# Four edits to the order of small work in a fused attention and mixer kernel: the pace of the weight sums, the engine of one cast, the slots of six stores, the slot of one unit

## The chip, the core and the metric

One core of a Trainium2 chip runs the whole kernel. The metric is the time of one execution in device microseconds (us), the median of several. A core has engines that run side by side, each through its own instructions in order: TensorE (PE; its weight loads are shown as PEld), VectorE (DVE), ScalarE (ACT), GpSimd (POOL), and SyncE (SP), which here only issues DMAs. They wait for each other by semaphores. TensorE writes its results to PSUM, a small memory from which VectorE and ScalarE read; everything else lies in SBUF.

## The reference

Local attention with a few global keys, and behind it a mixer: a low-rank product over the positions, then a feed-forward layer, both with a residual.

```python
batch, n_heads, seq, head_dim = (4, 8, 768, 64); n_global, n_local = (8, 96); rank = 32
# attention, for each batch and head
scores = q @ k.T / sqrt(64) - slope[h] * dist          # dist = distance, 96 for far global keys
scores = where(is_global | is_local, scores, -1e9)
x = softmax(scores) @ v                                 # -> [batch, 768, 512]
# mixer, for each batch
u = x + ((x.T @ U) @ V).T                               # U [768, 32], V [32, 768]
out = u + maximum(u @ w_ch1, 0) @ w_ch2                 # w_ch1 [512, 2048], w_ch2 [2048, 512]
```

## The kernel before

**Pairs.** The attention is done for two heads at a time: 4 batches of 4 such pairs, so pairs 0 to 15, pair `i` of batch `i // 4`. Pairs 0 to 3 (batch 0) run in a first loop. The main loop at the end of the function runs `i` from 4 to 17; in its turn `i` it does the scores of pair `i`, the product with v of pair `i - 1`, the mixer's low-rank step of pair `i - 1`, and it spreads "units" of the feed-forward layer between these steps. The order of every engine's instructions is that in which the code issues them.

**One turn of the main loop**, in its order on TensorE: scores in three parts (`st_S`, each freed for the next by VectorE's L403, which writes `sp`); between them the two halves of the product with v (`st_V`, VectorE's L437 and L451 behind it, then GpSimd's cast L452 of the result to `x16`); then `st_M1` (six matmuls, L461, x16 against U), whose small result is cast into a tile `turn16` (in the profile: `zw`) at L465; then `st_MT` (one matmul, L478, that turns it, read out at L479 into `tmp`); then `st_M3` (L515, against V, added to x at L520, after which GpSimd's L523 casts to x16); then `st_X`, a transposition by DMA (L504) of x16 into `uT`, which the feed-forward layer reads. In turns from 7 on SyncE also transposes the next pair's k and q (L327, L330). The exp of ScalarE (L415, two in a turn) needs all three parts of `sp`; ScalarE further casts k and q two pairs ahead (L129), once their loads have landed.

**Units.** `fill(n)` issues `n` units, at nine places in a turn, with the numbers of the tuple `units`. A unit is an "up" (eight matmuls, L629, u against w_ch1 into the accumulator `hps`, and a relu on ScalarE, L634) or a "down". For batch 0 a down is four matmuls of L664, and after four of these L669 adds to x. For the other batches the second product is done with seven products of sub-blocks instead of eight (L682, added at L687), for which sums of blocks are needed: sums of the activations (`s`, `htr`) for each group of 256 rows, and sums of the weights (`t1` to `t4`) once. Three PSUM accumulators rotate for `hps` and for the transposed q and k (tag "th"); the scores and M3 share one accumulator, and the product with v, M1 and MT share another.

**The weight sums.** `queue_weight_sums` puts ten VectorE operations (L553: six of 128x1024, four of 128x512) into the queue `slow`, each with a count of units from which it is due (`wait`); `fill` counts units and takes one due entry of `jobs` or else of `slow` behind each. They are queued when batch 0's second tile of rows begins, in turn 7.

**Stores.** A finished tile of 128 rows of x is stored by SyncE (L643). Batches 1 to 3 store at once. Batch 0's six stores are kept in `kept` and issued from turn 10 on, up to three a turn, ahead of `st_MT`; on SyncE's queue that is ahead of the turn's `st_X`.

Of the kernel before, what the change touches and what calls it, by code (L numbers as in the profile page):

```python
# [16 lines left out]
ALU = mybir.AluOpType  # L17
# [3 lines left out]
def kernel(  # L21
# [13 lines left out]
    nc = tc.nc  # L35
# [9 lines left out]
    R = moe_U.shape[1]  # L45
    NP = H // 2
    NPE = 2 * NP
# [36 lines left out]
    def ps_ob():  # L84
        return psum.tile([P, 512], FP32, name="ob", tag="ob", bufs=1)
# [4 lines left out]
    def ps_th(name, dtype=FP32, cols=512):  # L90
        return psum.tile([P, cols], dtype, name=name, tag="th", bufs=3)
# [5 lines left out]
    def load_qk(i, behind=None):  # L97

        b, h0 = i // NP, 2 * (i % NP)
        got = []  # L100
        for src, nm in ((q, "qst"), (k, "kst")):
            st = stp.tile([P, 2, NSB, D], FP32, name=nm, tag=nm, bufs=2)
            if behind is not None:
                behind.memset(st[0:1, 0, 0, 0:1], 0.0)
            if i < NPE:
                nc.sync.dma_start(
                    st.rearrange("p h n d -> p h (n d)"),
                    src[b, h0:h0 + 2].rearrange("h (p n) d -> p h (n d)", n=NSB),
                )
            else:  # L110
                nc.sync.dma_start(
                    st.rearrange("p h n d -> p (h n) d"),
                    src[b, h0:h0 + 2].rearrange("h (n p) d -> p (h n) d", p=P),
                )
            got.append(st)
        staged[i] = got
# [15 lines left out]
    def load_v(i):  # L132
        b, h0 = i // NP, 2 * (i % NP)
        st = stp.tile([P, 2 * NSB, D], FP32, name="vst", tag="vst", bufs=2)
        nc.sync.dma_start(
            st, v[b, h0:h0 + 2].rearrange("h (n p) d -> p (h n) d", p=P)
        )
        vsts[i] = st
# [84 lines left out]
    turn16 = [zw[:, i * P:(i + 1) * P] for i in range(2)]  # L223
# [11 lines left out]
    def new_batch(b):  # L235
        xs[b] = xp.tile([P, NSB, DM], FP32, name="x_sb", tag="x_sb", bufs=3)
        tmps[b] = xp.tile([P, DM], FP16, name="tmp16", tag="tmp16", bufs=3)
        uTs[b] = xp.tile([P, NDC, S], FP16, name="uT", tag="uT")
# [84 lines left out]
    def turn(i):  # L323
        stq, stk = cast.pop(i)
        qT = kp.tile([P, S], FP16, name="qT", tag="qT")
        kT = kp.tile([P, S], FP16, name="kT", tag="kT")
        nc.sync.dma_start_transpose(  # L327
            kT.rearrange("d (n p) -> d n p", n=NSB), stk.rearrange("p n h d -> p (n h d)")
        )
        nc.sync.dma_start_transpose(  # L330
            qT.rearrange("d (n p) -> d n p", n=NSB), stq.rearrange("p n h d -> p (n h d)")
        )
        qts[i] = qT
        kts[i] = kT
# [74 lines left out]
    def st_S(i, c):  # L409
        s_dve(i, scores(i, c, False))  # L410
# [44 lines left out]
    def st_M1(i):  # L455
        b, dc = i // NP, i % NP
        ch = slice(dc * P, (dc + 1) * P)
        if b:
            tps = ps_ob()
            for n in range(NSB):  # L460
                nc.tensor.matmul(  # L461
                    tps[:, 0:R], x16s[i][:, n], u16[:, n, 0:R],
                    start=(n == 0), stop=(n == NSB - 1),
                )
            nc.vector.tensor_copy(turn16[i % 2][:, 0:R], tps[:, 0:R])  # L465
            return
        tps = ps_th("tmp_ps")
        for n in range(NSB):
            nc.tensor.matmul(
                tps[:, 0:P], u16[:, n], x16s[i][:, n],  # L470
                start=(n == 0), stop=(n == NSB - 1),
            )
        nc.vector.tensor_copy(tmps[b][:, ch], tps[:, 0:P])
# [72 lines left out]
    jobs, slow = deque(), deque()  # L546
# [3 lines left out]
    def queue_sum(name, part, out_, a, b_, op, wait=0):  # L550

        def go():
            nc.vector.tensor_tensor(out_, a, b_, op)  # L553
            have.add((name, part))
        (slow if name[0] == "t" else jobs).append((count[0] + wait, go))
# [7 lines left out]
    def queue_weight_sums():  # L563

        t = wbig.tile([P, 3, HJ, HD], FP16, name="t16")
        b11, b12, b21, b22 = quarters
        dead = [slI[:, 0:4], slI[:, 4:8], rel16[:, 0:2], relB.bitcast(BF16)]
        dead = [d.bitcast(FP16) for d in dead]
        dead = [d if len(d.shape) == 2 else d.rearrange("p a c -> p (a c)") for d in dead]
        t3 = [d.rearrange("p (j c) -> p j c", j=2) for d in dead]  # L570
        tw.update(t1=t[:, 0], t2=t[:, 1], t3=t3, t4=t[:, 2])
        for name, a, b_ in (
            ("t1", b12, b11), ("t2", b22, tw["t1"]), ("t3", b22, b12), ("t4", b21, tw["t2"])
        ):
            for k in range(2 if name != "t3" else len(t3)):
                n = HJ // 2 if name != "t3" else HJ // len(t3)
                js = slice(k * n, (k + 1) * n)
                to = tw[name][:, js] if name != "t3" else t3[k]
                queue_sum(name, k, to, a[:, js], b_[:, js], ALU.subtract, wait=3 * len(slow))

    def weight(w, j):
        return tw[w][:, j] if w != "t3" else tw[w][j // 2][:, j % 2]
# [129 lines left out]
    ahead, held, kept = [0], [True], deque()  # L712

    def fill(n):
        for _ in range(n):
            unit()
            count[0] += 1
            for _ in range(2 if len(jobs) > 4 else 1):
                for queue in (jobs, slow):
                    if queue and queue[0][0] < count[0]:  # L720
                        queue.popleft()[1]()
                        break
# [77 lines left out]
    for i in range(NP, NPAIR + 2):  # L800
        b, hp = divmod(i, NP)
        live = i < NPAIR
        units = iter(
            (0, 1, 1, 2, 1, 1, 1, 1, 0) if i == NP
            else (0, 1, 1, 1, 1, 1, 1, 1, 1) if i + 1 < NPE
            else (1, 1, 1, 2, 1, 1, 1, 1, 1)
        )
        held[0] = i < NP + 3
        if hp == 0 and live and b + 1 < B:
            new_batch(b + 1)  # L810
        if live and i > NP:
            st_S(i, 0)
        if NPE <= i + 1 < NPAIR:
            turn(i + 1)
        if i + 1 < NPAIR and i != NP + 2:
            load_v(i + 1)
        if i + 2 < NPE:
            load_qk(i + 2)
        fill(next(units))
        if NPE + 2 <= i + 2 < NPAIR:  # L820
            cast_one(i + 2, 1, nc.scalar)
        if NP < i <= NPAIR:
            st_V(i - 1, 0)
        if i == NP:
            load_w1(2)
        if i + 1 < NPE:
            st_T(i + 1)
        if i == NP:
            load_w1(3)
        fill(next(units))  # L830
        if live:
            st_S(i, 1)
        fill(next(units))
        if NP < i <= NPAIR:
            st_V(i - 1, 1)
        if live:
            cast_v(i)
            st_A(i)
        if NPE + 2 <= i + 2 < NPAIR:
            cast_one(i + 2, 0, nc.scalar)  # L840
        if NPE <= i + 3 < NPAIR and i != NP + 2:
            load_qk(i + 3)
        if i > NP + 1 and (i - 2) % NP == NP - 1:
            queue_ff((i - 2) // NP)
            ahead[0] = 1
        if i == NPAIR + 1:
            break
        fill(next(units))
        if live:
            st_S(i, 2)  # L850
        fill(next(units))
        if i > NP:
            st_M1(i - 1)
        else:
            for xo, o, rb in later:
                nc.vector.tensor_tensor(xo, o, rb, ALU.mult)
        if i == NP + 1:
            load_w2(0)
            load_w2(1)
        if i + 2 < NPE:  # L860
            cast_qk(i + 2, nc.gpsimd)
        if live:
            st_E(i, 0)
            if i < NPE:
                st_P(i)
        fill(next(units))
        if i >= NPE + 2:
            for _ in range(min(3, len(kept))):
                kept.popleft()()
        if i > NP:  # L870
            st_MT(i - 1)
        if NPE <= i + 1 < NPAIR:
            st_K(i + 1)
        fill(next(units))
        if i > NP:
            st_M3(i - 1)
        if live:
            st_E(i, 1)
        fill(next(units))
        if i == NP + 1:  # L880
            load_v(i + 2)
            load_qk(i + 4)
        if i > NP:
            st_X(i - 1)
        if i == NP + 1:
            load_w2(2)
            load_w2(3)
        if NPE <= i + 2 < NPE + 2:
            cast_qk(i + 2, nc.gpsimd)
        fill(next(units))  # L890
# [38 lines left out]
```

## Time and profile before

| | us |
|---|---|
| median of 3 runs | 233.63 |
| the runs | 233.42, 233.63, 235.15 |
| the profiled execution, its own time | 234.27 |
| its span (first to last instruction) | 232.5 |

A turn as the profile times it, from one pair's first scores to the next's (busy time of the engines):

| pair | stretch, us | length | TensorE | VectorE | ScalarE | GpSimd |
|---|---|---|---|---|---|---|
| 8 | 73.5 to 85.1 | 11.60 | 11.60 | 9.31 | 4.80 | 5.12 |
| 9 | 85.1 to 96.5 | 11.40 | 11.40 | 9.03 | 6.15 | 2.68 |
| 10 | 96.5 to 108.8 | 12.30 | 11.53 | 11.25 | 8.86 | 3.47 |
| 11 | 108.8 to 120.2 | 11.40 | 11.31 | 9.68 | 6.97 | 2.82 |
| 12 | 120.2 to 131.4 | 11.20 | 11.20 | 9.69 | 7.88 | 2.23 |
| 13 | 131.4 to 144.7 | 13.30 | 11.71 | 10.24 | 7.97 | 3.34 |
| 14 | 144.7 to 156.2 | 11.50 | 11.37 | 10.08 | 6.16 | 2.82 |

The granted clock of TensorE is 1.0 throughout. The profile's rows give the start of an instruction from the span's start, its duration, the engine ("SPq" is SyncE's queue, where the time is that of issuing a DMA and not of its transfer), the line, the operation, what it writes and reads, and in square brackets how long the engine was idle before it and whose work ended that. Matmuls are pipelined, so a TensorE row overlaps the next one, and time is best read from start to start.

### The profile page before, as it was taken

How to read it: one execution, taken by the hardware profiler on the slowest of the kernel's cores; microseconds unless marked ns; L12 is line 12 of the kernel's file. 1: busy time of each engine (PE TensorE's matmuls, PEld its weight loads, DVE VectorE, ACT ScalarE, POOL GpSimd, SP SyncE). 2: the span in 40 equal slices, each digit the busy share in tenths (PEclk: the TensorE clock that was granted, in tenths of full speed). 3: DMA queues.
4: the chain of work that ended last, by engine and by line, in shares of the span. 5: the costliest groups of instructions: out<-in, count | busy, mean ns of one | idle time of the engine just before them, and what ended most of it. 6: DMA issues, size and time to landing. Idle time of an engine off the chain costs nothing.

```text
span 232.5 us, 5864 instructions
## 1 busy us (share of the span) xinstructions
PE 220.9 (95%) x2420; PEld 170.3 (73%) x2420; DVE 161.2 (69%) x349; ACT 123.9 (53%) x181; POOL 73.8 (32%) x118
## 2 busy tenths in 40 slices
PE   6899999899999999999999979999999999999994
PEld 2455678788745456877888858888998888888883
DVE  3687776759587968797979877979755444544452
ACT  6776857685705354957485738283633334333320
POOL 7399918297543413232313131222211000000000
PEclk9999999999999999999999999999999999999999
DMA  5999998969999978765999995861251202011022
GB/s 171 304 282 270 282 291 139 320 120 176 192 175 221 208 170 178 182 154 135 272 211 272 245 226 130 94 197 37 77 82 34 93 0 92 1 45 48 0 93 90
DMA packets 86562, 36.67 MB, mean 158 GB/s; under 512 B 74152, under 2 KB 83592, under 8 KB 86536
## 3 DMA queue, kind: packets, MB, share of 16 engines
q1 hardware_dynamic: 81480, 32.01, 57.5%
q0 software_dynamic: 5056, 4.29, 12.3%
q8 instruction: 19, 0.31, 0.6%
q14 instruction: 7, 0.06, 0.1%
HBM read 27.46 MB, written 6.29 MB: 145 GB/s over the span
## 4 chain that ended last, share of the span: by engine, by line
PE 68%; DVE 12%; DMA 8%; POOL 5%; ACT 2%; issue 1%; SPq 1%; DVEq 0%; POOLq 0%
PE hps L629 28%; PE cx L682 11%; PE cps L664 9%; PE cy L682 9%; DVE sp L403 4%; DMA vst<-in_v_dram 3%; PE sc L365 2%; DVE s L553 2%; DMA uT<-x 2%; DMA kT<-k 2%; PE sc L515 2%; PE ob L432 1%; DVE x_sb L687 1%; DVE htr L553 1%; PE ob L428 1%
## 5 line engine op out<-in xcount | busy, mean ns | idle before, releaser
L629 PE MATMUL hps<-uT,w 128*128 128x256 f16 x756 | 96.0, 273 | 1.4 <-DMA uT<-x 0.7
L634 ACT ACTIVATE htr<-hps 128x512 f16<-128x512 f32 x96 | 56.3, 597 | 60.4 <-PE hps L629 60.3
L629 PEld LDWEIGHTS <-w 128*128 128x128 f16 x756 | 70.6, 98 | 11.2 <-issue 1.6
L403 DVE SCALAR_TENSOR_TENSOR sp<-sc,relcat 128x1024 f32<-128x1024 f32 (+1 forms) x36 | 40.6, 1129 | 9.8 <-ACT ep L415 3.5
L415 ACT ACTIVATE ep<-sp 128x1408 f16<-128x1408 f32 x24 | 33.0, 1376 | 12.9 <-DVE sp L403 12.3
L452 POOL CAST x<-x_sb 128x384 f16<-128x384 f32 x30 | 16.4, 547 | 48.2 <-DVE x_sb L451 45.9
L682 PEld LDWEIGHTS <-htr 128*128 128x128 f16 x288 | 27.5, 98 | 4.7 <-ACT htr L634 1.1
L687 DVE TENSOR_TENSOR x_sb<-cx,x_sb 128x256 f32<-128x256 f32 x36 | 15.2, 422 | 18.1 <-PE cx L682 17.6
L523 POOL CAST x<-x_sb 128x768 f16<-128x768 f32 x12 | 10.9, 905 | 43.9 <-DVE x_sb L520 43.9
L664 PE MATMUL cps<-w,htr 128*128 128x512 f16 x96 | 24.0, 379 | 0.0
L682 PEld LDWEIGHTS <-s 128*128 128x128 f16 x216 | 20.3, 98 | 2.4
L687 DVE TENSOR_TENSOR x_sb<-cy,x_sb 128x256 f32<-128x256 f32 x27 | 11.4, 422 | 13.0 <-PE cy L682 12.7
L365 PEld LDWEIGHTS <-kT 64*128 64x128 f16 x192 | 8.3, 93 | 13.6 <-issue 12.2
L451 DVE TENSOR_TENSOR x_sb<-ob,rcp 128x384 f32<-128x384 f32 x30 | 16.7, 557 | 1.0
L365 PE MATMUL sc<-qT,kT 64*128 64x128 f16 x192 | 16.8, 221 | 0.0
L432 PE MATMUL ob<-v,ep 128*128 128x65 f16 x192 | 16.5, 193 | 0.0
L432 PEld LDWEIGHTS <-ep 128*128 128x128 f16 x192 | 13.9, 98 | 2.3 <-issue 0.3
L142 POOL CAST v<-vst 128x768 f16<-128x768 f32 x16 | 13.8, 865 | 3.9 <-DMA vst<-in_v_dram 3.9
L428 PE MATMUL ob<-vA,ep 128*128 128x65 f16 x160 | 14.4, 194 | 0.4 <-DVE vA L316 0.2
L520 DVE TENSOR_TENSOR x_sb<-sc,x_sb 128x768 f32<-128x768 f32 x12 | 11.5, 955 | 4.4 <-PE sc L515 4.4
L372 PE MATMUL sc<-qT,kA 64*128 64x128 f16 x160 | 14.3, 217 | 0.3
L664 PEld LDWEIGHTS <-htr 128*128 128x128 f16 x96 | 8.4, 97 | 8.0
(108 smaller groups left out, 310.8 us busy)
## 6 DMA issues: line engine op xcount, KB each, us to landing
qst<-in_q_dram SPq DMA_DIRECT2D x16, 384.0 KB, 5.5
kst<-in_k_dram SPq DMA_DIRECT2D x16, 384.0 KB, 5.6
vst<-in_v_dram SPq DMA_DIRECT2D x16, 384.0 KB, 3.9
out_dram<-x_sb SPq DMA_DIRECT2D x23, 256.0 KB, 3.5
w<-in_moe_w_ch_dram POOLq DMA_DIRECT2D x8, 512.0 KB, 8.0
vA<-v SPq DMA_DIRECT2D x8, 152.3 KB, 3.2
out_dram<-x_sb SPq DMA_DIRECT2D x2, 128.0 KB
uT<-x SPq DMA_TRANSPOSE x12, 3.6
```

The costliest lines, as they stand in the source:

```text
L365: nc.tensor.matmul(scs[hi][:, o:o + P], kT[r, kb * P:(kb + 1) * P], qT[r, kb * P:(kb + 1) * P], start=(o == 0 and not on_pe), stop=(o + P ...
L403: nc.vector.scalar_tensor_tensor(out=sps[i][:, :, c0:c0 + tot], in0=both[:, :, 0:tot], scalar=qk_scale / slope[2 * (i % NP)], in1=relfs[c0 ...
L415: nc.scalar.activation(eps[i][:, hi], sps[i][:, hi], AF.Exp, scale=slope[2 * (i % NP)])
L428: nc.tensor.matmul(ob[:, qi], ep[:, OF[qi - 1]:OF[qi - 1] + P], vA[:, qi - 1, hi], start=True, stop=False,)
L432: nc.tensor.matmul(ob[:, qi], ep[:, DG[qi]:DG[qi] + P], vt[:, qi, hi], start=(qi == 0), stop=True,)
L451: nc.vector.tensor_tensor(xo, ob[:, :, 0:D], rb, ALU.mult)
L452: nc.gpsimd.tensor_copy(x16, xo)
L629: nc.tensor.matmul(hps[:, k * FT:(k + 1) * FT], w1_16[:, dc, jt * P:(jt + 1) * P], uT[:, dc, ts], start=(dc == 0 and k == 0), stop=(dc == ...
L634: nc.scalar.activation(cell["htr"][:, 2 * jp:2 * jp + 2].rearrange("p j t -> p (j t)"), hps, AF.Relu)
L664: nc.tensor.matmul(cps, htr[:, jc, t * P:(t + 1) * P], w2_16[:, jc], start=(b > 0 and jc == 0), stop=(jc == NJC - 1),)
L682: nc.tensor.matmul(ps, cell[a][:, j], weight(w, j), start=(first and j == 0), stop=(done is not None and j == HJ - 1), skip_group_check=True,)
L687: nc.vector.tensor_tensor(x_sb[:, n, cs], ps, x_sb[:, n, cs], ALU.add)
```

## The change

Four edits, of which no one adds or removes arithmetic:

- `st_M1`'s cast at L465 (128x32, 12 in all) is issued on ScalarE instead of VectorE. On ScalarE it stands behind the relu of the unit ahead of M1 and ahead of the pair's first exp;
- the ten weight sums come due two units apart instead of three. In the order of VectorE's instructions the last of them moves from pair 10 to pair 9, and the earlier ones move up through pairs 7 to 9;
- batch 0's six stores are issued in turns 8, 9 and 10, up to two a turn. On SyncE's queue turns 8 to 11 have 2, 2, 2 and 0 of them where they had 0, 0, 3 and 3, each between the loads of q and k and the transposition L504;
- pair 4's turn asks for nine units instead of eight. On TensorE one up unit moves from the last slot of turn 6 to the last slot of turn 4; the order is otherwise as it was.

```diff
@@ -462,7 +462,7 @@
-            nc.vector.tensor_copy(turn16[i % 2][:, 0:R], tps[:, 0:R])
+            nc.scalar.copy(turn16[i % 2][:, 0:R], tps[:, 0:R])
             return
@@ -576,7 +576,7 @@
-                queue_sum(name, k, to, a[:, js], b_[:, js], ALU.subtract, wait=3 * len(slow))
+                queue_sum(name, k, to, a[:, js], b_[:, js], ALU.subtract, wait=2 * len(slow))
@@ -801,7 +801,7 @@
         units = iter(
-            (0, 1, 1, 2, 1, 1, 1, 1, 0) if i == NP
+            (0, 1, 1, 2, 1, 1, 1, 1, 1) if i == NP
             else (0, 1, 1, 1, 1, 1, 1, 1, 1) if i + 1 < NPE
             else (1, 1, 1, 2, 1, 1, 1, 1, 1)
         )
@@ -864,8 +864,8 @@
         fill(next(units))
-        if i >= NPE + 2:
-            for _ in range(min(3, len(kept))):
+        if i >= NPE:
+            for _ in range(min(2, len(kept))):
                 kept.popleft()()
         if i > NP:
             st_MT(i - 1)
```

## The prediction

> **What bounds the kernel now.** I read the page's first part, then TensorE's rows in order of time for each step longer than the same work takes elsewhere, then SyncE's and VectorE's rows for what it waited on.
>
> ```profile
> PE 220.9 (95%) x2420; PEld 170.3 (73%) x2420; DVE 161.2 (69%) x349; ACT 123.9 (53%) x181; POOL 73.8 (32%) x118
> ```
>
> TensorE is the bound, and the change takes no matmul away. Only its waits can go. A unit of eight 256-column matmuls steps on after 0.87 us (105.71 to 106.59 below), or 0.97 ahead of scores (90.19 to 91.16). Two stretches are worse (start, duration, engine, line):
>
> ```profile
> 102.63 1.05 PE L629 MATMUL hps<-uT,w 128*128 128x256 f16 x8
> 104.05 0.32 PE L461 MATMUL ob<-u,x 128*128 128x32 f16 x6 [0.37 <-POOL x L452]
> 104.21 1.03 PE L682 MATMUL cx<-t,s 128*128 128x256 f16 x8
> 105.65 0.23 PE L478 MATMUL ob<-ident,zw 128*128 128x128 f16 x1 [0.40 <-DVE zw L465]
> 105.71 1.04 PE L629 MATMUL hps<-uT,w 128*128 128x256 f16 x8
> 106.59 0.39 PE L515 MATMUL sc<-tmp,v16w 128*128 128x128 f16 x4
> ```
>
> ```profile
> 135.50 0.82 PE L682 MATMUL cy<-w,htr 128*128 128x256 f16 x6
> 137.18 0.39 PE L682 MATMUL cy<-w,htr 128*128 128x256 f16 x2 [0.86 <-ACT htr L634]
> 137.41 0.49 PE L629 MATMUL hps<-uT,w 128*128 128x256 f16 x3
> 138.63 0.71 PE L629 MATMUL hps<-uT,w 128*128 128x256 f16 x5 [0.74 <-DMA uT<-x]
> ```
>
> By steps the first stretch (pair 10) loses 0.55 (1.42 for 0.87) and 0.57 (1.44 for 0.87). The second (turn 13) loses 1.04 (135.50 to 137.41) and 0.89 (137.41 to the scores at 139.27, for 0.97). Four smaller losses sit behind L465 or L479: 0.26 at 117.11, 0.09 at 141.55, 0.29 at 153.04, 0.29 at 175.41. Together 3.98 us; that is nearly all there is to win after 66 us.
>
> SyncE's queue makes the second stretch:
>
> ```profile
> 108.05 2.92 SPq L643 DMA_DIRECT2D out_dram<-x_sb  x3
> ...
> 120.51 3.39 SPq L643 DMA_DIRECT2D out_dram<-x_sb  x4
> 124.00 1.47 SPq L504 DMA_TRANSPOSE uT<-x  x1
> ...
> 130.73 0.45 SPq L111 DMA_DIRECT2D qst<-in_q_dram  x1
> 131.24 0.80 SPq L111 DMA_DIRECT2D kst<-in_k_dram  x1
> 132.14 1.59 SPq L643 DMA_DIRECT2D out_dram<-x_sb  x1
> 133.84 1.30 SPq L504 DMA_TRANSPOSE uT<-x  x1
> ```
>
> The four stores before 124.00 hold back all that follows; SyncE hardly rests until 133.74. Pair 15's key load lands near 135.7, ScalarE's cast of it (135.79) holds a relu up, and the transposition from 133.84 lands at 138.59.
>
> **Ninth unit in pair 4: 0.** One unit (0.87) moves from pair 6's last slot to pair 4's. In pair 4 its relu (0.60) delays the next two: TensorE's 0.62 wait at 42.49 becomes about 0.45, so pairs 5 and 6 run some 0.5 later, and pair 7 gets 0.87 back. There one unit instead of two stands between M3's matmuls and the scores that reuse their bank; L520 (0.96) then costs about 0.2. What is left, 0.15, ends at the second-layer weights: the fourth part starts at 66.03, as the last of L230's four loads lands (issued 53.2, longest landing 12.8). Those issues follow a VectorE chain without idle from ScalarE's exp at 41.95, which the new unit doesn't move. If the loads did move, the cost is up to 0.5; the gain at most 0.15, from the wait there.
>
> **Cast on ScalarE: 12 VectorE casts of 0.18 go.** No row shows it on ScalarE; the nearest is L446 (128x64 from PSUM, 0.32), the lower bound VectorE's 0.18. I take 0.3. It stands ahead of the exp L415, which waits for the last scores anyway (VectorE 0.95), and behind the relu of the unit before it. Relu end plus 0.2 net meets MT where that relu starts late: pair 9 (93.11, MT 93.34) and turn 16 (173.97, MT 174.20) lose about 0.1 each. Exp comes 0 to 0.35 later; behind it are relus, whose accumulators have a slack of 0.3 (97.70 against 97.99). Gain: 0.26 + 0.09 + 0.29 + 0.29 = 0.93, cost 0.2 (0 to 0.8, if twelve).
>
> **Sums every two units.** Ten sums (six of 0.68, four of 0.41) now end near 91 instead of 102.6. Pair 10 loses two of 0.68 and the cast of 0.18; its VectorE had no idle from 95.75 to 106.53. But pair 9's exps come 0.2 later and set its first scores (97.21 plus 0.2 against 97.31), so its cast L479 (end 106.45) comes 0.68 + 0.09 - 0.15 = 0.6 earlier. TensorE could be 1.12 earlier, yet M3's matmuls need that cast: gain 0.6. Pairs 7 to 9 take the sums in. In pair 8 (VectorE 9.31 of 11.60 busy) two 0.41 sums go ahead of L451 and of sp's last part; L452's x then ends near 80.7 against M1 at 80.77: cost 0.1.
>
> One sum shows a bad case:
>
> ```profile
> 75.18 1.29 DVE L553 TENSOR_TENSOR t<-w,t 128x1024 f16<-128x1024 f16 x1
> ```
>
> It took 1.29 for 0.68 beside GpSimd's cast (75.10 to 75.93). The Trainium skill ("SBUF — State Buffer", Who interferes with whom) says why: a VectorE operation with two SBUF inputs and a GpSimd one that reads SBUF exclude each other for a whole instruction. By that rule, with which this row agrees, sums pulled to where GpSimd is busier cost more. GpSimd is busy 5.12 of 11.60 us in pair 8 and 3.47 of 12.30 in pair 10; the third rival below prices that from rows.
>
> **Stores in pairs 8 to 10.** Pairs 8, 9, 10, 11 issue 2, 2, 2, 0 of batch 0's six instead of 0, 0, 3, 3. A first store behind loads takes SyncE 1.4 to 1.95 (115.96: 1.41; 120.51: 1.61), a further one 0.44. Pair 11's three fewer, with 0.9 from VectorE's earlier pair 10, let the transposition of 124.00 go at about 121, pair 15's loads at about 128.7, the landing of pair 13's kT (VectorE waited 0.81 for it at 129.68) before its use. L520 and L687 end about 0.8 earlier, the store at about 131.6, the last transposition near 132.3; at 3.6 (median landing) it is there at 135.9, against a need (fourth matmul) near 136.2; at 4.8, as before, 137.1. I take 0.3 of the 1.93 as remaining: gain 1.64. The bounds are 0.4 and 1.93.
>
> The price is in pair 8:
>
> ```profile
> 83.76 0.69 SPq L111 DMA_DIRECT2D kst<-in_k_dram  x1
> 85.40 1.35 SPq L504 DMA_TRANSPOSE uT<-x  x1
> ```
>
> Two stores (1.95 + 0.44) between these push this transposition, batch 1's last, from 85.40 to 87.0. It landed 3.5 after issue, at 88.9; now 90.5, and 92.0 with the longest 5.0 (L504). The first batch 1 unit starts at 90.19 and needs it 0.33 later. Cost 0.25 (0 to 1.5). kT, qT and v behind it wait no longer than vA did anyway (GpSimd's cast of v, 91.83). In pair 9, SyncE was idle from 94.86 to 97.14, which covers two stores.
>
> **Sum:** 0.93 + 0.6 + 1.64 - 0.2 - 0.1 - 0.25 = 2.62. The profiled execution took 234.27 (span 232.5 and 1.77 around it), above the median of 233.63; its waits are taken as the median's, so 231.65 for it and 231.0 for the median. A measurement can tell about 1% (2.34 us) from no change.
>
> **Rivals.**
> - The last transposition stays tied to TensorE: it follows M3 (129.25), L520, a store that must wait for L687, and lands 4.8 after, whatever SyncE's queue. For: 133.84 came 0.1 after the store, and that 1.8 after L687. Against: 0.81 of L520's lateness was kT's. The gain there is 0.4: 233.63 - 1.38 = 232.25. Chance 0.25.
> - Pair 8's transposition becomes the bound. L504's first issue held SyncE for 10.04 at 56.13, while loads filled the DMA queue; behind two stores it could be held half as long. Then it lands near 95, TensorE stands still some 4.5 more than I took, and the change loses: 233.63 - 2.62 + 4.5 = 235.5 (238 with a longer hold). It decides from a landing of 93.4 on. Against: after three stores the one at 111.08 took 1.44. Chance 0.12.
> - Sums meet GpSimd's casts in pair 8: two more at the 0.6 extra of 75.18 make M1 late by up to 1.2: 232.2. Chance 0.13.
> - The order of instructions shows all four edits, so they do what they say; that the ninth unit moves the weight loads (0.5: 231.5) has 0.05.
>
> **Numbers.** The forecast has 0.45, with its own range of 230.2 to 232.3: all 3.98 but 0.5 gives 230.2, the full 1.5 in pair 8 gives 232.3. The whole range takes in the first and third rival and goes to no change, 230.0 to 233.6. Faster by over 1% (below 231.3) is some seven tenths of the forecast (0.32) and 0.09 of the others, 0.41; slower by over 1% is the second rival's worse half and a little beyond, 0.08; 0.51 lies between.
>
> **What would show it.** Right: no wait on zw at L478; L461 in pair 10 without its 0.37; the wait for uT near 137 gone or under 0.5; pair 11's transposition issued near 121; under 0.5 at the first batch 1 unit. Wrong: a wait for uT near 90 over 1 us, or the one near 137 still over 1 us.

## The result, and the profile after

| | before | after |
|---|---|---|
| median, us | 234.04 (7 runs, 233.42 to 235.15) | 232.05 (7 runs, 231.41 to 232.49) |
| ratio of the medians, 95% interval | | 0.9908 [0.9883, 0.9933] |
| the profiled execution | 234.27 | 231.95 |
| its span | 232.5 | 230.2 |
| end of the last matmul, from the span's start | 229.18 | 226.47 |
| from there to the end of the span | 3.31 | 3.71 |

The change makes the kernel 0.9% faster: 1.99 us between the medians, 2.3 us between the two profiled executions. The two last rows already hold a surprise: TensorE ends 2.71 us earlier, and 0.40 of it is lost behind TensorE.

The first part of the page after:

```profile
span 230.2 us, 5875 instructions
PE 220.5 (96%) x2418; PEld 171.1 (74%) x2420; DVE 159.8 (69%) x337; ACT 124.8 (54%) x193; POOL 73.9 (32%) x118
```

TensorE is busy as long as before within the 0.4 us that two missing matmul records and pipelining leave; what went is its waiting. VectorE has twelve instructions fewer and ScalarE twelve more: the casts of L465.

TensorE's rows after, in order of time, where the losses were and where new ones stand (start, duration, engine, line; the idle time before a row in brackets):

```profile
66.12 1.02 PE L664 MATMUL cps<-w,htr 128*128 128x512 f16 x4 [0.43 <-DMA w<-in_moe_w_ch_dram]
...
90.25 1.18 PE L629 MATMUL hps<-uT,w 128*128 128x256 f16 x8
91.35 0.23 PE L365 MATMUL sc<-qT,kT 64*128 64x128 f16 x2
...
102.83 1.05 PE L629 MATMUL hps<-uT,w 128*128 128x256 f16 x8
103.71 0.30 PE L461 MATMUL ob<-u,x 128*128 128x32 f16 x6
103.86 1.03 PE L682 MATMUL cx<-t,s 128*128 128x256 f16 x8
104.73 0.22 PE L478 MATMUL ob<-ident,zw 128*128 128x128 f16 x1
104.79 1.04 PE L629 MATMUL hps<-uT,w 128*128 128x256 f16 x8
106.03 0.50 PE L515 MATMUL sc<-tmp,v16w 128*128 128x128 f16 x6 [0.21 <-DVE tmp L479]
...
134.67 1.03 PE L682 MATMUL cy<-w,htr 128*128 128x256 f16 x8
135.54 1.04 PE L629 MATMUL hps<-uT,w 128*128 128x256 f16 x8
136.51 0.23 PE L365 MATMUL sc<-qT,kT 64*128 64x128 f16 x2
...
137.68 0.61 PE L682 MATMUL cx<-t,s 128*128 128x256 f16 x4 [0.28 <-DVE s L553]
```

Pair 10: both steps of a unit are 0.87 again (102.83 to 103.71, 103.86 to 104.73), and M1 and MT wait for nothing. A new wait of 0.21 stands at M3. Turn 13: the unit at 134.67 steps on after 0.87 and the next after 0.97; the waits of 0.86 and 0.74 are gone. A new wait of 0.28 stands behind the scores. The wait at 66.12 is new too, and it will turn out to belong to more than the change.

SyncE's rows after, for pair 8 and for the queue that made turn 13 late:

```profile
84.71 2.08 SPq L643 DMA_DIRECT2D out_dram<-x_sb  x2
86.90 1.29 SPq L504 DMA_TRANSPOSE uT<-x  x1
...
119.40 1.85 SPq L643 DMA_DIRECT2D out_dram<-x_sb  x1
121.35 1.28 SPq L504 DMA_TRANSPOSE uT<-x  x1
...
129.62 1.63 SPq L643 DMA_DIRECT2D out_dram<-x_sb  x1
131.34 1.29 SPq L504 DMA_TRANSPOSE uT<-x  x1
```

One store instead of four stands before pair 11's transposition, which goes at 121.35 instead of 124.00, and the last one at 131.34 instead of 133.84.

**The ledger.** Each step of TensorE is set against the same step before; a change of the shift is a gain or a loss at that place.

| place | change of the shift, us |
|---|---|
| up to the weights' wait at 66 | +0.10 |
| first unit of batch 1 (90.25) | +0.14 |
| pair 10: M1, MT, then M3 | -0.53, -0.57, +0.37 |
| MT at 116.30 | -0.26 |
| turn 13: second product, up unit, then the first product's second half | -1.03, -0.90, +0.46 |
| MT at 139.15 and 150.35 | -0.09, -0.29 |
| M3 at 172.70 (175.41 before) | 0 |
| behind the last matmul | +0.40 |

The rows from 90 to 172 make a gain of 2.70, against 2.62 predicted from all terms together.

### The profile page after: what moved, and what is told of

Its sections match the earlier page's. It is cut to its first block, busy times and chain, and to the rows that moved or that the text cites. A ratio compares the mean times of both kernels' runs of the same rounds, so it can differ in the third digit from the quotient of the medians.

```text
span 230.2 us, 5875 instructions
## 1 busy us (share of the span) xinstructions
PE 220.5 (96%) x2418; PEld 171.1 (74%) x2420; DVE 159.8 (69%) x337; ACT 124.8 (54%) x193; POOL 73.9 (32%) x118
## 4 chain that ended last, share of the span: by engine, by line
PE 66%; DMA 11%; DVE 10%; POOL 4%; ACT 4%; issue 2%; SPq 1%; ACTq 0%; POOLq 0%
PE hps L629 25%; PE cx L682 13%; PE cy L682 10%; PE cps L664 8%; DMA w<-in_moe_w_ch_dram 6%; DMA vst<-in_v_dram 4%; DVE sp L403 3%; PE sc L365 3%; DMA qst<-in_q_dram 2%; ACT ep L415 2%; DVE x_sb L451 2%; PE ob L432 2%; PE sc L515 1%; DVE s L553 1%; PE ob L428 1%
## 5 line engine op out<-in xcount | busy, mean ns | idle before, releaser
L629 PE MATMUL hps<-uT,w 128*128 128x256 f16 x756 | 96.0, 273 | 0.0
L629 PEld LDWEIGHTS <-w 128*128 128x128 f16 x756 | 70.6, 98 | 9.9 <-issue 0.2
L687 DVE TENSOR_TENSOR x_sb<-cx,x_sb 128x256 f32<-128x256 f32 x36 | 15.2, 422 | 18.3 <-PE cx L682 17.7
L664 PE MATMUL cps<-w,htr 128*128 128x512 f16 x96 | 24.0, 379 | 0.4 <-DMA w<-in_moe_w_ch_dram 0.4
L687 DVE TENSOR_TENSOR x_sb<-cy,x_sb 128x256 f32<-128x256 f32 x27 | 11.4, 422 | 12.5 <-PE cy L682 12.3
L664 PEld LDWEIGHTS <-htr 128*128 128x128 f16 x96 | 8.4, 97 | 8.5 <-issue 0.5
L520 DVE TENSOR_TENSOR x_sb<-sc,x_sb 128x768 f32<-128x768 f32 x12 | 11.5, 955 | 4.6 <-PE sc L515 4.6
```

What stands on the lines that cost most here:

```text
L629: nc.tensor.matmul(hps[:, k * FT:(k + 1) * FT], w1_16[:, dc, jt * P:(jt + 1) * P], uT[:, dc, ts], start=(dc == 0 and k == 0), stop=(dc == ...
L664: nc.tensor.matmul(cps, htr[:, jc, t * P:(t + 1) * P], w2_16[:, jc], start=(b > 0 and jc == 0), stop=(jc == NJC - 1),)
L687: nc.vector.tensor_tensor(x_sb[:, n, cs], ps, x_sb[:, n, cs], ALU.add)
```

## The experiments

In each run "rest" is the time from the fourth part of L664 (66.12 above) to the end of the last matmul, from that kernel's trace: 163.16 before, 160.35 after. It leaves out what happens ahead of 66 us, which differs from execution to execution, as is shown below. Each rest is that of one profile, so it tells where a kernel gains or loses, and a few tenths between two of them prove nothing by themselves.

### One edit undone

Stores back in their old slots:

```diff
-        if i >= NPE:
-            for _ in range(min(2, len(kept))):
+        if i >= NPE + 2:
+            for _ in range(min(3, len(kept))):
```

> The changed kernel with batch 0's six stores back in turns 10 and 11, three each; the other three edits stay. Theory (SyncE's queue): turn 13's two waits come back, because four stores again stand ahead of turn 11's transposition; the last transposition of batch 2 is issued after 132.5 and TensorE waits over 1 us for uT near 137; the first batch 1 unit loses its 0.14 at 90.25. Time 0.8 to 1.5 us above the changed kernel, ratio to before 0.994 to 0.998. Rival (VectorE's relief in pair 10 alone moved turn 13): no wait over 0.3 us near 137, time within 0.3 us of the changed kernel, ratio 0.990.

Measured: 234.63 (12 runs; the kernel before, run beside it, 235.40, 17 runs), ratio 0.9961 [0.9924, 0.9999]; rest 162.09, 1.74 longer than after. SyncE's rows:

```profile
119.08 3.24 SPq L643 DMA_DIRECT2D out_dram<-x_sb  x4
122.42 1.83 SPq L504 DMA_TRANSPOSE uT<-x  x1
...
132.93 1.29 SPq L504 DMA_TRANSPOSE uT<-x  x1
```

Four stores are ahead of pair 11's transposition again. The last transposition goes 1.6 later than after, though TensorE is 0.47 earlier in this execution, and TensorE waits for vA (0.33), a relu (0.64) and uT (0.89, a little less than the 1 us expected) in turns 12 and 13. The first unit of batch 1 takes no longer step here. So it is the store edit that frees turn 13.

Eight units, the cast on VectorE, and the sums every three units, each alone in the changed kernel:

```diff
-            (0, 1, 1, 2, 1, 1, 1, 1, 1) if i == NP
+            (0, 1, 1, 2, 1, 1, 1, 1, 0) if i == NP
```

> The changed kernel with eight units in pair 4's turn. Theory: the fourth part of the first tile's second product starts at 66.0 to 66.15 as in both kernels, since the weights' landing sets it, and everything after it is unmoved: time within 0.2 us of the changed kernel, ratio 0.990 to 0.991. Rival (the ninth unit is worth its wait at 42.5): 0.4 to 0.6 us slower.

```diff
-            nc.scalar.copy(turn16[i % 2][:, 0:R], tps[:, 0:R])
+            nc.vector.tensor_copy(turn16[i % 2][:, 0:R], tps[:, 0:R])
```

> The changed kernel with the cast at L465 back on VectorE. Theory: L478 waits for it again by 0.2 to 0.3 us each near 117, 139 to 141 and 150 to 153 and by up to 0.3 in pair 10, where L479 sets the end anyway: 0.5 to 0.9 us slower than the changed kernel, ratio 0.993 to 0.995. Rival (the sums' pace alone cleared VectorE's queue): within 0.2 us.

```diff
-                queue_sum(..., ALU.subtract, wait=2 * len(slow))
+                queue_sum(..., ALU.subtract, wait=3 * len(slow))
```

> The changed kernel with the weight sums due every three units. Theory: pair 10 has two sums of 0.68 again; L461's wait for GpSimd's cast (0.4 to 0.55 by steps) and a wait for L479 come back: 0.5 to 0.8 us slower than the changed kernel, ratio 0.993 to 0.994; SyncE's loads for pair 15 come later, but no wait over 0.5 us near 137. Rival (the cast's move alone cleared pair 10): within 0.2 us.

| in the changed kernel | median, us (6 runs each) | ratio | rest | against 160.35 |
|---|---|---|---|---|
| eight units | 232.28 | 0.9846 [0.9803, 0.9890] | 160.23 | -0.12 |
| cast on VectorE | 232.37 | 0.9865 [0.9821, 0.9910] | 161.04 | +0.69 |
| sums every three | 232.50 | 0.9881 [0.9843, 0.9919] | 160.85 | +0.50 |

These ran beside the kernel above. None can be told from another by its time. The changed kernel's own 0.9908 is from other runs, in which the kernel before read 234.04, so they do not count as faster than it. All three ratios lie below those expected (0.990 to 0.991, 0.993 to 0.995 and 0.993 to 0.994), so the times confirm none of the three prices. The traces, one of each kernel, tell more. With the cast on VectorE MT waits for zw again (0.28, 0.09 and 0.13) and the steps lose 0.45 in pair 10 (0.37 of it comes back at M3, whose wait is then absent), then 0.25, 0.16 and 0.29. With the slower pace M1 in pair 10 is 0.56 later. The eight units lose nothing after 66 us. All three are 0.14 ahead at the first unit of batch 1, which is in step again. Ahead of 66 us the three profiles differ, most at this row of the eight units:

```profile
66.79 1.02 PE L664 MATMUL cps<-w,htr 128*128 128x512 f16 x4 [1.73 <-DMA w<-in_moe_w_ch_dram]
```

### One edit alone

The four edits as in the change, each put alone into the kernel before: the stores, the unit, the cast, the pace.

> The kernel before with the stores' edit alone. Theory (SyncE's queue): pair 10 loses its 1.12 us as before, and the first batch 1 unit 0.14; but pair 11's transposition goes earlier than 124.0 by 1 to 2 us, and turn 13's 1.93 falls to 0.3 to 0.9: ratio to before 0.994 to 0.997 (0.8 to 1.5 us). Rival (VectorE's relief moved turn 13): 1.000 or slower.

> The kernel before with the ninth unit alone. Theory: the fourth part of the first tile still starts at 66.0 to 66.15, ratio 0.999 to 1.001. Rival: a gain of 0.4 to 0.6 us, ratio 0.998.

> The kernel before with the cast alone on ScalarE. Theory: what it wins ahead of turn 13 (0.57 less what L479 takes back in pair 10, 0.26 at 117) is waited out again at turn 13, where uT lands when SyncE lets it; what it wins behind stays (0.09 and 0.29): ratio 0.997 to 0.999 (0.3 to 0.6 us). Rival (the waits add up wherever they are): 0.9 us or more, ratio 0.996 or less.

> The kernel before with the sums every two units alone. Theory: pair 10 ends 0.3 to 0.6 us earlier, and turn 13 takes most of it back, since SyncE's queue is full from 120 to 134: ratio 0.997 to 1.000. Rival (pair 10 frees SyncE's queue too, by 0.9 us, and that reaches turn 13): ratio 0.995 or less, and a wait for uT under 0.4 us near 137.

| in the kernel before | median, us | ratio | rest | against 163.16 |
|---|---|---|---|---|
| stores | 233.52 (10 runs) | 0.9922 [0.9894, 0.9950] | 162.05 | -1.11 |
| unit | 234.53 (12) | 0.9966 [0.9937, 0.9995] | 163.22 | +0.06 |
| cast | 235.04 (12) | 0.9993 [0.9961, 1.0024] | 165.15 | +1.99 |
| pace | 235.32 (12) | 1.0003 [0.9972, 1.0034] | 164.11 | +0.95 |

(Before, run beside these: 235.14, 33 runs.) The product of the four ratios is 0.9884; the change has 0.9908 [0.9883, 0.9933]. The stores alone bring most of it. In their trace both waits of turn 13 go whole (steps 1.02 and 0.90 shorter), where 0.3 to 0.9 was expected to stay, and the new wait behind the scores stands there too (0.45 lost); pair 11's transposition goes at 121.07. So turn 13 is freed without anything that VectorE gains in pair 10. The unit alone, expected at 0.999 to 1.001, reads 0.6 us faster, with nothing of it behind 66 us. The cast and the pace bring nothing by themselves, and the trace of the cast alone says where its gain goes:

```profile
120.99 0.20 PE L428 MATMUL ob<-vA,ep 128*128 128x65 f16 x1 [0.56 <-DMA vA<-v]
132.36 0.23 PE L365 MATMUL sc<-qT,kT 64*128 64x128 f16 x2 [1.33 <-DVE x_sb L520]
134.39 0.19 PE L428 MATMUL ob<-vA,ep 128*128 128x65 f16 x1 [0.62 <-DMA vA<-v]
```

SyncE's rows of the same kernel:

```profile
120.49 3.35 SPq L643 DMA_DIRECT2D out_dram<-x_sb  x4
123.93 1.97 SPq L504 DMA_TRANSPOSE uT<-x  x1
126.02 2.59 SPq L327 DMA_TRANSPOSE kT<-k  x1
```

With the four stores still there, the transposition of k was issued at 126.02 and took SyncE 2.59, where it took 1.22 from 125.57 before; VectorE waits 2.21 for kT there (0.81 before), and the 1.33 for L520 follows from that. Turns 12 and 13 wait for what SyncE sends: in all 4.0 us with a relu (0.61) and uT (0.88), against 1.60 before. In the other kernels with late stores these waits come to 1.44 (unit alone), 1.86 (stores late) and 3.04 (pace alone). So a profile with late stores can lose there more than the cast and the pace bring; whether by the kernel or by the execution, one profile of each can't say, and it stays open. The times show that the cast and the pace bring nothing measurable while the queue is full; the traces above, one of each kernel, have them bring something once it is free.

### The weights' landing, and the ninth unit without it

The wait at 66 us is for the last of L230's four loads. The first two of these are moved from turn 5 to the end of turn 4, the other two to where the first two were; in the changed kernel, in the kernel before, and in the changed kernel with eight units:

```diff
         if i == NP + 1:
-            load_w2(0)
-            load_w2(1)
+            load_w2(2)
+            load_w2(3)
         if i + 2 < NPE:
...
             st_X(i - 1)
-        if i == NP + 1:
-            load_w2(2)
-            load_w2(3)
+        if i == NP:
+            load_w2(0)
+            load_w2(1)
```

> The changed kernel, with the first two of L230's loads moved from turn 5 to the end of turn 4 (issued near 39.9 instead of 48.7) and the other two to where the first two were (48.7 instead of 52.5). Theory: the landing of the last of these loads decides when TensorE passes 66 us, differs by execution (64.9 to 67.6 in the ten profiles so far) and so makes much of the spread. Then no wait for w at the fourth part of L664, which starts at 65.2 to 65.8; from there to the last matmul 160.3 as in the changed kernel; span 229.6; ratio to before 0.985 to 0.989, where the changed kernel has 0.991. Rival: the loads are only moved onto the loads of the first-layer weights and of q, k and v, and TensorE or VectorE waits for one of those instead (an idle stretch of over 0.4 us put down to a DMA between 40 and 64): ratio 0.991 or above.

> The kernel before, with the same move of L230's loads and nothing else. Theory: what they cost has nothing to do with the change; the fourth part of L664 starts at 65.3 to 65.9 with no wait for w, from there to the last matmul 163.2 as before; ratio 0.995 to 0.999. Rival: in the kernel before TensorE is held at 66 us by something else as well, and the start stays at 66.0 or above: ratio 1.000.

> The changed kernel with L230's loads moved in the same way and with eight units in pair 4's slot, as before. It prices the ninth unit where no landing covers it. My prediction gave it at most 0.15 gained (the 0.62 wait at 42.49 less 0.39, less 0.24 behind L520). By that the fourth part of L664 starts 0.0 to 0.2 later than with nine units and the ratio is within 0.002 of that kernel's. Rival: the gap behind L520 costs more than the wait at 42.49, and eight units start the fourth part 0.2 or more earlier.

| loads early | median, us | ratio | rest |
|---|---|---|---|
| changed kernel | 230.46 (5 runs, 230.15 to 230.95) | 0.9814 [0.9794, 0.9834] | 160.21 |
| kernel before | 234.40 (12 runs) | 0.9970 [0.9942, 0.9998] | 163.90 |
| changed, eight units | 231.04 (6 runs) | 0.9840 [0.9815, 0.9865] | 160.51 |

(Before, run beside these: 234.97, 17 runs.) The changed kernel with early loads is the best of all, 4.5 us below the kernel before and 1.9% faster, which is more than was expected (ratio 0.985 to 0.989). The changed kernel itself did not run beside it. Its fourth part of L664 has no wait, and starts at 64.44 where 65.2 to 65.8 was expected, as this execution's first unit is early (32.72):

```profile
63.23 1.04 PE L664 MATMUL cps<-w,htr 128*128 128x512 f16 x4
64.44 1.02 PE L664 MATMUL cps<-w,htr 128*128 128x512 f16 x4
```

The last of the four loads lands at 59.31 here, 5.1 us ahead of its use. What the move is worth shows when the profiles of all fourteen kernels are laid side by side. Worked out from TensorE's rows: the start of the first up unit (L629), the time from there to the fourth part of L664, the wait just ahead of that part, and the time without it.

| kernel | units in pair 4, loads | first unit | to 4th part | wait | without it |
|---|---|---|---|---|---|
| before | 8, late | 33.78 | 32.24 | 0 | 32.24 |
| stores alone | 8, late | 32.91 | 32.25 | 0 | 32.25 |
| cast alone | 8, late | 32.85 | 32.39 | 0.14 | 32.25 |
| pace alone | 8, late | 33.75 | 33.66 | 1.42 | 32.24 |
| changed, eight units | 8, late | 32.81 | 33.97 | 1.73 | 32.24 |
| unit alone | 9, late | 32.86 | 33.32 | 1.44 | 31.88 |
| after | 9, late | 33.80 | 32.32 | 0.43 | 31.89 |
| stores late | 9, late | 33.24 | 32.54 | 0.67 | 31.87 |
| cast on VectorE | 9, late | 32.81 | 32.08 | 0.20 | 31.88 |
| sums every three | 9, late | 34.40 | 33.16 | 1.28 | 31.88 |
| stores in 9 to 11 (below) | 9, late | 33.06 | 32.42 | 0.54 | 31.88 |
| before, early loads | 8, early | 33.68 | 32.09 | 0 | 32.09 |
| changed, eight, early | 8, early | 33.91 | 32.08 | 0 | 32.08 |
| changed, early | 9, early | 32.72 | 31.72 | 0 | 31.72 |

Three things are apart now. The first unit starts anywhere from 32.7 to 34.4, ahead of every edit: that is how far executions differ up to there. The last load of the weights lands early enough or up to 1.7 us too late, with both 8 and 9 units; moved ahead, it is late in none of three profiles, which saves the wait and 0.15 or 0.16 more at the same step. And without the wait the stretch is 32.24 with eight units and 31.88 with nine: the ninth unit is worth 0.36 us, with late loads and with early ones, and the landing takes it away where it is later than TensorE. In the row of the kernel with eight units and early loads the wait is still there that the unit fills:

```profile
42.62 1.03 PE L629 MATMUL hps<-uT,w 128*128 128x256 f16 x8 [0.62 <-ACT htr L634]
```

SyncE is held for long in either case, by another issue: 9.3 to 11.2 us at the first transposition L504 (from 56.47 after) in the eleven kernels with late loads, and 8.9 to 9.0 at a load of v (from 46.92 in the changed kernel) in the three with early ones, where no L504 takes more than 2.1. So the hold moves with the loads of the weights.

I had expected 0 to 0.2 of the unit, the rival a loss; both fall. The medians of the two changed kernels with early loads differ by 0.58 in the same direction, their intervals just overlap. In the kernel before the time and the start of the fourth part (65.77) came out as the theory had it, but its rest was 163.90 instead of 163.2: turns 12 and 13 waited 0.65 for vA, 0.58 for a relu and 0.92 for uT, 2.15 in all, as kernels with late stores do.

### The stores one turn later

Batch 0's stores in the slots of pairs 9, 10 and 11, two in each:

```diff
-        if i >= NPE:
+        if i >= NPE + 1:
             for _ in range(min(2, len(kept))):
```

> The changed kernel with batch 0's six stores in the slots of pairs 9, 10 and 11, two in each, instead of 8, 9 and 10. Theory: what the store edit gains is SyncE's free queue in pair 11, and what it costs is the transposition of pair 8. So the first unit of batch 1 (near 90) loses its wait of 0.13, pair 11's transposition goes at 122.3 instead of 121.4, the last one near 133 instead of 131.3, and turn 13 loses 0.3 to 0.9; from L664's fourth part to the last matmul 160.5 to 161.1 instead of 160.35; ratio 0.991 to 0.994. Rival: only three stores or more in pair 11 fill the queue, two do not; then turn 13 is as in the changed kernel, 160.2 and the same ratio or 0.001 below.

Measured: 232.16 (6 runs), ratio 0.9885 [0.9855, 0.9916] run beside the kernels with early loads; rest 160.49, 0.14 longer than after. SyncE's rows:

```profile
118.87 2.63 SPq L643 DMA_DIRECT2D out_dram<-x_sb  x3
121.60 1.29 SPq L504 DMA_TRANSPOSE uT<-x  x1
...
131.97 1.29 SPq L504 DMA_TRANSPOSE uT<-x  x1
```

The longer step of batch 1's first unit (1.10 after, 91.35 less 90.25) is 0.97 here: with no store in pair 8 the transposition is issued earlier. In the seven kernels with two stores there that step is 0.14 longer in one (after), 0.29 in two and not at all in four, so it lands just on time. From 91 to 135 this execution runs 0.78 ahead of the profile of after. Against TensorE, then, two more stores in pair 11 send its transposition 1.0 later (121.60 and 0.78 against 121.35) and the last one 1.4, close to the 122.3 and 133 of the theory; turn 13 loses 0.63 to a relu behind a late key load, and 0.36 comes back as the new wait behind the scores is absent. In the trace the theory holds, at its low end (160.5 was the least expected); the ratio, 0.9885, is below the 0.991 to 0.994 that it gave. As the two places nearly cancel, neither slot is better than the other by a time that shows.

## Why the prediction was right

The forecast was 231.0 with a range of 230.0 to 233.6; the time is 232.05. As differences that is 2.6 predicted against 2.0 between the medians and 2.3 between the profiled executions, since the kernel before read 234.04 beside the runs of after. The five signs of being right that it named are all in the rows. The largest term of the sum was right in place and mechanism, the second in three of its four places. That the terms measured add up to 2.60, nearly the 2.62 of the forecast, is in part luck, as misses on both sides cancel; the sizes stand beside them:

- **Stores, 1.64 predicted, 1.47 measured.** Pair 11's transposition went at 121.35 (about 121 said), pair 15's loads at 128.31 (about 128.7), the last transposition at 131.34 (near 132.3, so a microsecond too cautious), and the wait for uT is gone, not 0.3. The 1.93 was won whole, and by SyncE's queue alone: the 0.9 from VectorE's earlier pair 10, which the term counts in, was not needed, as the stores alone win it too. What was missed is the 0.46 behind it: a new wait for the sum `s` of L553. VectorE's rows there:

```profile
136.08 0.57 DVE L553 TENSOR_TENSOR s<-htr 128x512 f16<-128x512 f16 x1
136.69 0.94 DVE L553 TENSOR_TENSOR s<-s,htr 128x512 f16<-128x512 f16 x1
```

GpSimd's:

```profile
135.87 0.51 POOL L452 CAST x<-x_sb 128x384 f16<-128x384 f32 x1 [1.93 <-DVE x_sb L451]
136.32 1.03 POOL L142 CAST v<-vst 128x768 f16<-128x768 f32 x1
```

The two sums of the activations took 0.57 and 0.94 where they took 0.41 and 0.42 before, and GpSimd's cast of v 1.03 instead of 0.84. Before, TensorE was late here, and the sums (137.95, 138.40) came as GpSimd had ended (138.01). Now they fall together with it. The waits that hid it were taken away. With the stores alone the same rows read 0.57, 0.93 and 1.03. This is the third rival's mechanism at another place: in pair 8, for which it was written, the sums pulled ahead ran undisturbed (0.41 and 0.42) and the one at 75.24 took 1.12, no worse than 1.29 before; in turn 13 it cost 0.46. The rule of the Trainium skill ("SBUF — State Buffer", Who interferes with whom), that a VectorE operation with two SBUF inputs and a GpSimd one that reads SBUF shut each other out, agrees with these rows; no run here separates it from another cause.

- **Cast on ScalarE, 0.93 less 0.2 predicted; 0.64 and no cost measured.** The cast's rows, after and before (shortest, median and longest in ns):

```profile
L465 ACT CAST zw<-ob x12: 179/180/187, 48.3 to 171.2; 128x32 f16<-128x32 f32 x12
```

```profile
L465 DVE CAST zw<-ob x12: 175/182/193, 47.6 to 173.6; 128x32 f16<-128x32 f32 x12
```

ScalarE needs 0.18, the lower bound, not the 0.3 taken, and the stalls of 0.1 in pair 9 and turn 16 did not come. The 0.26, 0.09 and 0.29 were won as said. The fourth, 0.29 at 175.41, was not; it was put to the wrong cause. The row had said so: what stands still there reads `tmp` of L479, not `zw`. VectorE before, there, and TensorE's row:

```profile
173.63 0.18 DVE L465 CAST zw<-ob 128x32 f16<-128x32 f32 x1
174.40 0.42 DVE L687 TENSOR_TENSOR x_sb<-cx,x_sb 128x256 f32<-128x256 f32 x1 [0.58 <-PE cx L682]
174.74 0.42 DVE L553 TENSOR_TENSOR htr<-htr 128x512 f16<-128x512 f16 x1
175.07 0.28 DVE L479 CAST tmp<-ob 128x128 f16<-128x128 f32 x1
175.41 0.27 PE L515 MATMUL sc<-tmp,v16w 128*128 128x128 f16 x2
```

VectorE idles between the first two. What keeps L479 is the order: it stands behind L687 and L553, and L687 waits for TensorE.

- **Sums every two, 0.6 predicted, 0.73 measured in pair 10**: 1.10 at M1 and MT, 0.37 back at M3 for its cast L479. The pace frees M1 (undone, it is 0.56 later) and the cast MT (undone, 0.45 later, of which 0.37 comes back at M3). M1 in pair 8 lost nothing (0.1 said).
- **Stores in pair 8, 0.25 predicted, 0.14 measured.** The transposition went at 86.90 (87.0 said). It lands just on time: in the changed kernel with early loads it was issued 0.18 earlier against TensorE, and the step was not longer; with eight units and early loads it was issued 0.09 earlier but took SyncE 1.77 instead of 1.29, and the step was 0.29 longer.
- **Ninth unit, 0 predicted, 0.10 lost here.** The reason given was half right: the landing does end it, in this execution with a wait of 0.43. But what it would be worth without that is 0.36, not 0.15: the wait of 0.62 at 42.49, of which 0.45 was to stay, goes whole; 0.24 of it comes back at the step just ahead of it, and 0.24 behind L520 (about 0.2 said). The fourth rival, that the unit moves these loads, falls: they are issued at 48.71 and 52.49, where it was 48.70 and 52.48.
- **Behind the last matmul, nothing predicted, 0.40 lost.** This is the only part of the result that no step looked at.

The terms make 1.47 + 0.64 + 0.73 - 0.14 - 0.10 = 2.60 up to the last matmul, 0.1 less than the 2.71 between the two traces (steps under 0.04 are left out), and 2.3 after the 0.40. The two rivals at 232.2 and 232.25 lie nearest to the median in their numbers, by other mechanisms than they named: the last transposition did move with SyncE's queue, by 2.5 us where TensorE was only 0.8 earlier, and M1 in pair 8 was not late. The rival that had pair 8's transposition held for long needed a landing after 93.4, and it is there before the first unit's scores at 91.35.

## What to carry to other kernels

A queue that is full in one turn can be emptied into turns that have idle time on it, and the small gains elsewhere (a cast moved, sums pulled ahead) brought nothing that showed here while that queue ended the wait. Before a term is put to an edit, read which tile the waiting row names: a wait for the next cast in the chain is not won by moving the one before. Where a load's landing sits close to its first use, look at it in several executions: here it was free in one and cost 1.7 us in another. Issuing it one slot earlier brought about as much in the kernel before (0.9970) as the best of the three small edits (the unit, 0.9966).

## What was not expected of the hardware

The 0.40 behind the last matmul is in every kernel with stores in pairs 8 to 10 and in no other. From the traces, SyncE's own instructions near the end, waits for semaphores among them, counted from 0:

```
                 SyncE's instructions   last matmul to end   idle ahead of its instruction no. 207
before and the five others with the old slots   208     3.30 to 3.32   0.45 or 0.46, its last one
stores in pairs 9 to 11                         209     3.46           0.39
after and the six others with pairs 8 to 10     213     3.71 to 3.72   0.36 or 0.37
```

The last bytes arrive and their semaphore is seen at the same distance behind the last matmul in all of them. Then SyncE stands still for 0.36 to 0.39 us ahead of its instruction 207 in the streams of 209 and 213, where that is a DRAIN and a wait. Before, it is the last instruction, ahead of which SyncE waits for the others anyway (0.45 or 0.46 with 213 too, ahead of number 212). With 213 it is one of the waits at the end, ahead of which SyncE idles 0.03 in the kernel before, and five more instructions stand behind it. The stores in pairs 8 to 10 bring a net five more waits into SyncE's stream and so, it seems, move that place into the path. Two things in the traces fit a place that goes by the number and has to do with the loading of instructions. In all fourteen the last 8 KB packet of the instruction queue q14 starts 0.56 to 0.88 us behind the start of number 207, even where that lies behind the span's end. And 128 instructions earlier, ahead of number 79, SyncE idles 0.44 or 0.45 us in the seven kernels with 213, and again such a packet follows, 0.6 to 1.0 us behind. That this is what stops the engine is not shown, as no kernel was built to move the place.

A second one: executions differ by up to 1.7 us in when the first unit starts, and by as much in how late a 512 KB load lands. The kernel with early loads had the narrowest spread, 0.8 us over five runs; beside it the one with stores in pairs 9 to 11 had 2.2 over six.
